# First norm, DFT stage, kernel spectrum and convolution slices put into one list schedule, with the tables' second half by quarters

## The chip, the cores and the metric

The kernel runs on one core of a Trainium2 chip. Times are device microseconds (us) of one execution; the time of a kernel is the median over its runs. A profiled execution gives a trace beside its time; positions in it are in us from the start of its span.

## What is computed

Four layers are added to a residual `x` of 2048 tokens by 512 channels, in bf16: a state-space convolution (A), a dilated sliding attention (B), A again and B again, each on a layer-normed input and each with the same weights in both rounds.

```python
def _A_ref(u, A_re, A_im, B_re, B_im, C_re, C_im, log_dt, Dskip):
    ...
    P = jnp.exp(logdA[:, :, None] * l[None, None, :])
    K = jnp.einsum("dn,dnl,dn->dl", Cc, P, dB).real
    ...
    Yf = Uf * Kf[None, :, :, :]
    ...
    y = (lambda x, *d: x.transpose(*d))(y, 0, 2, 1) + u * Dskip[None, None, :]
    return y
...
x = A_u
x = x + _A_ref(_layernorm(x, axis=-1), ...)
x = x + _B_ref(_layernorm(x, axis=-1), B_wqkv, B_wo)
x = x + _A_ref(_layernorm(x, axis=-1), ...)
x = x + _B_ref(_layernorm(x, axis=-1), B_wqkv, B_wo)
return x
```

A is a long convolution by FFT with a kernel `K` of 2048 lags for each channel, a sum over 128 complex modes. B has 32 heads of 16, each token looking at 8 keys, 2 tokens apart.

## The kernel before

**Front: the convolution's kernel (`kgen`, from L345).** `_kgen_ladder` raises the modes' factors to the powers 1, 2, 4 to 2048 (`Lb`). From these VectorE multiplies out two tables, `V` (32 multiples of 8 lags) and `U` (21 offsets): for each complex product four multiplications and two sums (`cmul`, L322). The 512 channels are done in two halves, the half in two blocks of 128 channels (blocks 0 to 3). In the first half TensorE adds the products up in PSUM (`psadd`, L473 and L474) and ScalarE writes the table back (L475); in the second half VectorE does the sums too. For each block, `products` (L418) multiplies V by U on TensorE (`psk`, four groups of 32 matmuls), ScalarE copies the result to `KT`, and small transfers put it in order (`rows`, eight of 20 KB, L442, for blocks 2 and 3 half of them issued by ScalarE). `spectrum` (L448) multiplies `rows` by a DFT matrix `G` (`psg`, four steps `b` of ten matmuls for each block), ScalarE evicts to `ks`, and SyncE stores it to the DRAM scratch `kt_scratch` (L457, 256 KB each).

**First norm.** ScalarE takes sums and squares of the 16 row groups (`first_norm_stats`, L165), handed out a few at a time by `norm_stats`; four of the squares come behind block 2's evictions. After the last table operation VectorE applies the norm, 16 operations (`first_norm_apply`, L188).

**First convolution (`a_layer`, L240).** `first_stage` (L218) is the first DFT stage: 16 steps of two matmuls (`ps_s`), set in turns with the last spectrum steps by hand, evicted to `Z` by ScalarE and VectorE in turn. Then 16 slices of 32 channels run in a fixed software pipeline (loop at L283): TensorE transposes (`pt`), VectorE evicts (`zt`), TensorE runs the second stage (`xp`), ScalarE evicts (`xc`), VectorE multiplies by the kernel's spectrum (`pab`, L294), TensorE inverts (`vp`), ScalarE evicts to `VT` (L279). A slice's spectrum `Kt` is loaded by SyncE as two transfers of 256 KB into one of four buffers; slice `cg + 4` is issued once the product of slice `cg` has read its buffer. The matrix of the inverse's last stage, `F1T`, has its own tile and is loaded before slice 0. The last lag (`kU`, L304 and L306) comes after the last slice. Then the first attention layer begins with the rows of the result (`y_rows`, `ps_y`).

**Attention (`b_layer`, L677) and the scheduler.** `Plan` (L616) takes operations with an engine, an estimated duration, what they follow and which buffer they take and give back, and emits them at trace time: again and again the operation with the earliest start, the first in the list among equals. An operation counts as done 0.2 us (`LAG`) after its end, for every engine. In the before kernel only `b_layer` is made by it. Each engine then runs its list in that order; semaphores hold it where something is not ready. The second convolution uses `a_layer` again, with `Z` made by the first attention layer's end.

## Time and profile before

| | us |
|---|---|
| runs | 498.71, 503.98, 503.78 |
| median | 503.78 |
| profiled execution, its time | 499.52 |
| its span | 497.7 |

| stretch of the span | from | to | length |
|---|---|---|---|
| loads, ladder, start of the tables | 0 | 42.0 | 42.0 |
| tables, first half | 42.0 | 64.6 | 22.6 |
| tables, second half | 64.6 | 110.8 | 46.2 |
| first norm applied, first DFT stage, rest of the spectrum | 110.8 | 144.5 | 33.7 |
| slices of the first convolution | 144.5 | 181.2 | 36.7 |
| first attention, with the second layer's DFT stage | 181.2 | 326.4 | 145.2 |
| slices of the second convolution | 326.4 | 363.4 | 37.0 |
| second attention, store | 363.4 | 497.7 | 134.3 |

Busy over the whole span: TensorE 401.0 us (81%), VectorE 421.8 (85%), ScalarE 339.0 (68%). Each engine works through its own list; what an engine waits for is put down to the semaphore that came last. The chain of waits follows the execution back from its last instruction, at each step to what released it. The DMA share is the mean busy share of the core's 16 DMA engines.

### The profile page before, as it was taken

How to read it: one execution, taken by the hardware profiler on the slowest of the kernel's cores; microseconds unless marked ns; L12 is line 12 of the kernel's file. 1: busy time of each engine (PE TensorE's matmuls, PEld its weight loads, DVE VectorE, ACT ScalarE, POOL GpSimd, SP SyncE). 2: the span in 40 equal slices, each digit the busy share in tenths (PEclk: the TensorE clock that was granted, in tenths of full speed). 3: DMA queues.
4: the chain of work that ended last, by engine and by line, in shares of the span. 5: the costliest groups of instructions: out<-in, count | busy, mean ns of one | idle time of the engine just before them, and what ended most of it. 6: DMA issues, size and time to landing. Idle time of an engine off the chain costs nothing.

```text
span 497.7 us, 11589 instructions
## 1 busy us (share of the span) xinstructions
PE 401.0 (81%) x4760; PEld 261.9 (53%) x4760; DVE 421.8 (85%) x842; ACT 339.0 (68%) x571; POOL 4.6 (1%) x19
## 2 busy tenths in 40 slices
PE   2008789959979979999876798779889998957896
PEld 1003366446437844685664565258645674845663
DVE  4999999995458969895999999978788886999980
ACT  5987988665658968768552279769868667733244
POOL 3000000000000000000000000000000000000000
PEclk9999975979999999999995699999999999975699
DMA  8910001633669970037073003529800073080022
GB/s 255 426 81 0 2 1 28 121 63 71 163 151 279 258 209 2 1 88 147 3 151 82 2 3 79 175 78 238 196 1 1 4 159 75 19 199 19 1 85 86
DMA packets 38404, 49.85 MB, mean 100 GB/s; under 512 B 27936, under 2 KB 29216, under 8 KB 37456
## 3 DMA queue, kind: packets, MB, share of 16 engines
q1 hardware_dynamic: 35488, 45.81, 35.6%
q10 hardware_dynamic: 2704, 3.18, 2.6%
q8 instruction: 37, 0.61, 0.5%
q0 software_dynamic: 160, 0.13, 0.1%
q14 instruction: 15, 0.12, 0.1%
HBM read 30.67 MB, written 6.29 MB: 74 GB/s over the span
## 4 chain that ended last, share of the span: by engine, by line
PE 37%; DVE 21%; DMA 10%; ACT 5%; issue 3%; ACTq 1%; SPq 1%; DVEq 0%
DVE prodqk L836 9%; PE ps_qk L808 7%; DMA Kt<-kt_scratch 6%; DVE prodpv L959 5%; PE ps_o L989 5%; PE po L966 4%; DMA V<-c_zero 4%; PE psg L451 3%; PE ps_v L862 3%; DVE pab L294 2%; ACT xc L287 2%; PE ps_y L317 2%; PE ps_y L313 1%; PE pt_x L793 1%; PE Lp L848 1%
## 5 line engine op out<-in xcount | busy, mean ns | idle before, releaser
L836 DVE TENSOR_TENSOR prodqk<-qT,kT 128x1024 bf16<-128x1024 bf16 (+3 forms) x176 | 83.0, 537 | 4.8 <-ACT kT L810 2.6
L959 DVE TENSOR_TENSOR prodpv<-V,Lsb 128x1024 bf16<-128x1024 bf16 (+2 forms) x128 | 79.6, 680 | 4.9 <-DMA V<-c_zero 3.2
L808 PE MATMUL ps_qk<-xnT,wqk 128*128 128x512 bf16 x256 | 60.9, 379 | 0.0
L966 PE MATMUL po<-halves,prodpv 128*128 128x64 bf16 x1024 | 50.2, 208 | 8.6 <-DVE prodpv L959 6.0
L966 PEld LDWEIGHTS <-prodpv 128*128 128x128 bf16 x1024 | 42.8, 107 | 19.4 <-DVE prodpv L959 12.3
L294 DVE TENSOR_TENSOR pab<-xc,Kt 128x2048 bf16<-128x2048 bf16 x32 | 39.2, 1224 | 8.8 <-DMA Kt<-kt_scratch 6.8
L451 PE MATMUL psg<-G,rows 128*128 128x512 bf16 x160 | 39.8, 408 | 6.1 <-DMA rows<-KT 6.1
L473 PE MATMUL psadd<-cp,sb_ident 128*128 128x512 bf16 (+3 forms) x48 | 18.1, 378 | 31.8 <-DVE cp L332 28.7
L848 PE MATMUL Lp<-sb_bones,prodqk 128*128 128x8 bf16 x1024 | 32.6, 167 | 11.6 <-DVE prodqk L836 11.2
L848 PEld LDWEIGHTS <-prodqk 128*128 128x128 bf16 x1024 | 30.7, 97 | 17.5 <-DVE prodqk L836 14.5
L277 PE MATMUL vp<-sb_IC,pab 128*128 128x128 bf16 x512 | 33.9, 219 | 3.5 <-DVE pab L294 3.5
L279 ACT CAST VT<-vp 128x1024 bf16<-128x1024 f32 x32 | 32.5, 1016 | 6.1 <-PE vp L277 6.1
L287 ACT CAST xc<-xp 128x1024 bf16<-128x1024 f32 x32 | 32.6, 1020 | 5.7 <-PE xp L210 5.7
L808 PEld LDWEIGHTS <-wqk 128*128 128x128 bf16 x256 | 23.4, 97 | 22.8 <-issue 0.5
L332 DVE TENSOR_TENSOR cp<-Vtab,L 128x896 bf16<-128x896 bf16 (+6 forms) x64 | 34.1, 596 | 0.4 <-PE psadd L474 0.4
L989 PE MATMUL ps_o<-wo_t,oT 128*128 128x512 bf16 x128 | 33.0, 379 | 0.0
L277 PEld LDWEIGHTS <-pab 128*128 128x128 bf16 x512 | 29.8, 98 | 5.4 <-DVE pab L294 4.7
L764 DVE BATCH_NORM_STATS2 ln_stats<-X 128x6 f32<-128x512 bf16 x44 | 28.6, 677 | 4.6 <-ACT X L1021 4.6
L978 ACT CAST oT<-po 128x512 bf16<-128x512 f32 x32 | 17.3, 586 | 21.2 <-PE po L966 21.1
L451 PEld LDWEIGHTS <-rows 128*128 128x128 bf16 x160 | 16.4, 103 | 27.8 <-issue 10.8
L862 PE MATMUL ps_v<-wv,xnT 128*128 128x256 bf16 x256 | 30.9, 272 | 0.0
L332 DVE TENSOR_TENSOR cp<-Utab,L 128x256 bf16<-128x256 bf16 (+4 forms) x60 | 29.3, 548 | 0.9 <-PE psadd L474 0.8
(152 smaller groups left out, 752.5 us busy)
## 6 DMA issues: line engine op xcount, KB each, us to landing
Kt<-kt_scratch SPq DMA_DIRECT2D x64, 256.0 KB
V<-V SPq DMA_DIRECT2D x22, 256.0 KB
G<-c_G SPq DMA_DIRECT2D x4, 1280.0 KB
kt_scratch<-ks SPq DMA_DIRECT2D x16, 256.0 KB
X<-in_A_u_dram SPq DMA_DIRECT2D x4, 512.0 KB
F1Tsb<-c_F1T SPq DMA_DIRECT2D x2, 1024.0 KB
V<-V SPq DMA_DIRECT2D x4, 441.0 KB
F1sb<-c_F SPq DMA_DIRECT2D x1, 1024.0 KB
```

The lines of the kernel that those rows point to most:

```text
L277: nc.tensor.matmul(vp[:, g, :], pab[:, g, ab, :], IC[:, ab, :], start=(ab == 0), stop=(ab == 1))
L287: nc.scalar.copy(xc[:].rearrange("q g o l -> q (g o l)"), xp)
L294: last = nc.vector.tensor_tensor(pab[:], xc[:].to_broadcast([128, 8, 2, 128]), kts[cg][:], ALU.mult)
L332: nc.vector.tensor_tensor(prod[i, r].rearrange("n (h e t) -> n h e t", h=hn, t=2), a(r), m[:, i].unsqueeze(2).to_broadcast([128, hn, e, 2] ...
L451: mms = [nc.tensor.matmul(ps[:, hf, :], rows[:, t, :], Gt[b][:, t, hf * 512:(hf + 1) * 512], start=(t == 0), stop=(t == 4)) for t in range ...
L808: nc.tensor.matmul(t.ps[:], wqk[:, ct, f0:f0 + 128], xnT[g][:, ct, :], start=(ct == 0), stop=(ct == 3))
L836: nc.vector.tensor_tensor(b.pr[:, u:u + 2 * n, a, :], cols(qT[i][:, ja * 128:(ja + n) * 128]), cols(kT[i][:, k0:k0 + n * 128]), ALU.mult)
L848: nc.tensor.matmul(t.Lp[:, w, u % 2, u // 2, :], b.pr[:, u].rearrange("f a q -> f (a q)"), bones[:], start=True, stop=True)
L862: nc.tensor.matmul(t.ps[:, jj, :], xnT[jp // 2][:, ct, c0:c0 + 128], wv[:, ct, fp * 256:(fp + 1) * 256], start=(jj + ct == 0), stop=(jj == ...
L959: nc.vector.tensor_tensor(t.p2[:, 0:nj, :].rearrange("p j (d h) -> p j d h", d=DH), m.V2[i // 2][:, c, r0:r0 + nj, f0:f0 + 128].rearrange( ...
L966: nc.tensor.matmul(po[jj // k][:, jj % k, c - cs[0], :], t.p2[:, jj, :], fold, start=(c == cs[0] and w == 0 and jj % k == 0), stop=(c == c ...
L989: nc.tensor.matmul(t["ps"][:], m.oT[:, ft, j * 128:(j + 1) * 128], wo_t[:, ft, :], start=(ft == 0), stop=False)
```

## The change

The functions `kgen` and the first use of `a_layer` become one function, `front`; `a_layer`'s second use becomes `second_conv`.

- **One list.** From the first half's fifth table step on, everything up to the first convolution's last slice is put into a `Plan`: table steps, products, rows, spectrum, stores, the first norm, the DFT stage, Kt loads, slices, `F1T`, last lag, and the loads of the attention's weights. Hand-made turns are gone. An operation can have a rank; among equal starts the lowest rank goes first. The products (`psk`) of blocks 1 to 3, the norm's applies and the DFT stage's first half share one rank, behind block 0's operations and ahead of block 1's spectrum, of all that follows for blocks 2 and 3, and of the second half's tables; slice `cg` has 100000 + 1000 `cg`, and block 3's four spectrum steps the ranks of slices 4, 6, 8 and 10.
- **Quarters.** In the second half of the tables U_4, U_2 and U_2048 are done for the half; U_1, U_256, U_1024 and U_512 for each block, followed by that block's V. The V16 step is cut in two for each block.
- **Engines.** Half of the norm's applies go to ScalarE. `Z` is made in two halves of 256 channels: the first evicted by ScalarE alone, the second by ScalarE or VectorE as the list finds it. So are `zt`, `xc` and `VT` of the slices.
- **Memory.** U of the first half and one product buffer lie in an arena; after the last reader, the normed rows and the first half of `Z` take it, and in the attention layers `oT` takes the place of `Z`. The slices' buffers, `VT` and the second half of `Z` take the tables' memory after block 3's last product (`done`). All four `G` tiles lie where the ladder's work was. `Kt` has three buffers in the first convolution, four in the second. `F1` and `F1T` share one buffer: `F1T` is loaded after the DFT stage (first convolution: after Kt load 9; second: after Kt load 5), and `F1` once more in the first attention layer.
- **Scheduler.** `Plan` counts an operation as done at its end for the same engine and after the lag for others; a lag can be given (3.0 for Kt loads and stores, 2.4 for rows). This holds for the attention layers too.

```diff
@@ Plan @@
-    def add(self, eng, us, fn, after=(), take=None, drop=()):
+    def add(self, eng, us, fn, after=(), take=None, drop=(), lag=None, rank=None):
...
+    def seen(d, eng):
+
+        return d["end"] + (0.0 if d["eng"] == eng and d["lag"] == Plan.LAG else d["lag"])
...
-        taken, left = {}, list(self.ops)
+        taken, left = {}, sorted(self.ops, key=lambda o: (o["rank"], o["k"]))
@@ first norm @@
-def first_norm_apply(nc, st, Xg, Ng):
-    for j in range(NJ):
-        nc.vector.tensor_scalar(Ng[j // 4][:, j % 4, :], Xg[j // 4][:, j % 4, :], st["rstd"][:, j:j + 1],
-                                st["nb"][:, j:j + 1], ALU.mult, ALU.add)
+    return [plan.add(dict(ACT=0.71) if j % 2 else dict(DVE=0.324), None, lambda eng, j=j: apply(eng, j), [o, room], rank=rank) for j in range(NJ)], sums
@@ slices @@
-        for cg in range(4):
-            load_k(cg)
...
+        k = plan.add("SP", 1.3, load, [room] + stored(cg), take=("Kt", m.kts), lag=3.0, rank=rank)
...
+        a = plan.add("PE", 0.46, turn, [room] + ready(cg), take=PT, rank=rank)
+        b = plan.add(dict(ACT=0.93, DVE=0.61), None, turned, [a], take=("zt", 3), drop=[a], rank=rank)
+        c = plan.add("PE", 0.44, second, [b], take=PX, drop=[b], rank=rank)
+        d = plan.add(dict(ACT=0.92, DVE=1.15), None, spectrum, [c], take=("xc", 2), drop=[c], rank=rank)
+        e = plan.add("DVE", 1.14, product, [d, k], take=("pab", 4), drop=[d, k], rank=rank)
...
+        f = plan.add("PE", 1.03, inverse, [e], take=PS, drop=[e], rank=rank)
...
+        ends.append(plan.add(dict(ACT=0.92, DVE=1.15), None, inversed, [f], drop=[f], rank=rank))
+    for cg in range(16):
+        rank = 100000 + 1000 * cg
+        slice32(cg)
+    for cg in range(14):
+        inverses[cg]["after"].append(seconds[cg + 2])
@@ second_conv @@
+        m = SimpleNamespace(z=lambda h: Z[:, h * 64:(h + 1) * 64], kts=4)
...
+        plan.add("SP", 0.65, load_f1t, loads[5:6], rank=0)
+        last_lag(nc, plan, m, C, Ng, ends[11:12])
@@ front: tables, second half @@
-        U = u_start(1)
-        for step in (U_4, U_2, U_1, U_256, U_1024, U_512, U_2048):
-            u_last = u_mul(1, U, *step)
...
+        products(0)
+        rank1 = len(plan.ops)
+        products(1)
+        start = [plan.add("DVE", 0.35, lambda: u_start(1))]
+        for st in (U_4, U_2, U_2048):
+            start = dve_step(u_mul(1, cp[:], *st), start)
+        for q, (h0, h1) in enumerate(quarters):
+            o = start
+            for st in (U_1, U_256, U_1024, U_512):
+                o = dve_step(u_mul(1, cp[:], *st, h0, h1), o)
...
+            for k in (2, 4, 8):
+                o = dve_step(v_mul(1, cp[:], k, h0, h1), o)
+            for i in range(2):
+                e = (h1 - h0) // 2
+                o = dve_step(v_mul(1, cp[:], 16, h0 + i * e, h0 + (i + 1) * e), o)
+                got["tab", 2 + q, 2 * i] = got["tab", 2 + q, 2 * i + 1] = o
+            if q:
+                rank_g.update({(3, b): 100000 + 1000 * (4 + 2 * b) for b in range(4)})
+            products(2 + q)
@@ front: products and spectrum in the list @@
+                p = plan.add("PE", 1.08, pe, need + (got["rows", c - 2] if c > 1 else []), take=PS if q % 2 else PX, rank=rank1 if c else None)
...
+                p = plan.add("PE", 2.16, pe, got["moved", c], rank=rank, take=PS, drop=[r0] if b == 3 else ())
+                o = plan.add("ACT", 0.92, evict, [p], take=("ks", 2), drop=[p], rank=rank)
+                got["stored", c].append(plan.add("SP", 0.65, store, [o], drop=[o], lag=3.0, rank=rank))
@@ front: norm, memory, DFT stage @@
+        room = plan.add("-", 0.0, arena, [p for ps, _ in half0 for p in ps] + [got["psk", c, q][0] for c in range(2) for q in range(4)])
+        normed, sums = first_norm(nc, plan, C, Xg, Ng, room, cpp.tile([128, D], BF, name="junk"), rank1)
...
+        done = plan.add("-", 0.0, tables_done, [got["psk", 3, q][0] for q in range(4)] + sums)
...
+                p = plan.add("PE", 0.23, pe, [normed[j]] + ([done] if hf else []), take=PX if j % 3 == 2 else PT, rank=None if hf else rank1)
...
+                got["Z", hf].append(plan.add(dict(ACT=act_us(512), DVE=0.68) if hf else dict(ACT=act_us(512)), None, evict, [p], drop=[p], rank=None if hf else rank1))
+        m.z = lambda h: m.Z[h]
+        loads, ends = conv_slices(nc, plan, m, C, kt_dram, lambda cg: got["Z", cg // 8], lambda cg: got["stored", cg // 4], done)
+        last_lag(nc, plan, m, C, Ng, [done] + got["rows", 3])
...
+        plan.add("SP", 0.65, f1t, s1 + [loads[9]])
@@ b_layer @@
-            m.oT = m.vo.tile([128, 4, S], BF, name="oT")
+            m.oT = C["arena2"].rearrange("f (i s) -> f i s", i=4)
+            if not last_layer:
+                C["F1"] = C["f1"].tile([128, NJ, 2, 128], BF, name="F1", tag="F1")
...
+        if not last_layer:
+            plan.add("SP", 0.65, lambda: nc.sync.dma_start(C["F1"][:], C["F1_h"].ap()), [y_end])
```

## The prediction

> **What bounds the kernel now.** I first read the busy time by stages, since the change rewrites only the work up to the first convolution's end (181.2 us); the rest it touches only through the scheduler's rule and two table loads. The columns are the stretch, its length, then busy time of TensorE, its weight loads, VectorE (DVE), ScalarE (ACT) and GpSimd, the granted clock, the DMA share and GB/s.
>
> ```profile
> 64.60:110.80 46.20, 38.46 (x463) 25.52 (x463) 46.17 (x101) 33.08 (x63) 0.00 (x0) 0.77 0.31 58
> 110.80:144.50 33.70, 30.85 (x249) 15.46 (x250) 16.00 (x35) 20.74 (x26) 0.21 (x1) 0.96 0.53 123
> 144.50:181.20 36.70, 30.75 (x417) 25.15 (x416) 31.13 (x36) 31.37 (x33) 0.00 (x0) 1.00 0.97 259
> ...
> 326.40:363.40 37.00, 30.93 (x416) 25.10 (x417) 31.16 (x36) 30.34 (x32) 0.00 (x0) 1.00 0.73 172
> ```
>
> From 64.6 to 110.8 VectorE is full: it multiplies out the tables' second half. From 110.8 to 144.5 VectorE has 16.0 of 33.7 us; nothing else is ready for it. In both convolutions (third and fourth line) no engine is full, but the DMA share of the first is 0.97. The chain of waits says what ends last there:
>
> ```profile
> 108.54 1.88 DMA rows<-KT
> ...
> 110.76 5.84 PE psg L451 x20
> ...
> 126.19 2.16 PE psg L451 x10
> ...
> 142.49 2.16 PE psg L451 x10
> ...
> 159.09 1.24 DVE pab L294
> 160.34 0.51 SPq L259
> ...
> 160.91 6.57 DMA Kt<-kt_scratch
> ...
> 177.81 1.24 DVE pab L294
> ```
>
> After the tables the chain runs over the rows' transfer, then through TensorE's spectrum (psg, 2.16 us for ten matmuls) and the first DFT stage in turns, and from 159 through Kt loads: a product (pab) frees a buffer, the next load is issued and lands 6.57 us later. How fast that stream can be, the windows of ten microseconds show:
>
> ```profile
> 90.00:100.00 10.00, 10.00 (x48) 4.52 (x47) 10.00 (x22) 5.77 (x7) 0.00 (x0) 1.00 0.67 132
> ...
> 160.00:170.00 10.00, 9.45 (x134) 7.85 (x132) 8.58 (x11) 9.63 (x12) 0.00 (x0) 1.00 1.04 261
> 170.00:180.00 10.00, 7.82 (x113) 6.50 (x111) 7.84 (x8) 8.42 (x9) 0.00 (x0) 1.00 1.04 284
> ```
>
> At a full share (1.04) Kt loads move 261 GB/s (the third line has the weights in it too); so 512 KB, one slice, take 2.0 us, the pace of the products (pab at 161.98 to 177.81: eight slices in 15.8). In the first line only spectrum stores ran, one per 2.16 us at a share of 0.67: 1.45 us of all engines each.
>
> **The change part by part.** All is worked against the profiled execution: span 497.7, time 499.52. The median of the three runs is 503.78, 4.26 above, so the difference found is taken off the median.
>
> *Tables by quarters.* Four U steps and each V16 step are cut in two: (4 + 2) x 6 = 36 more instructions on VectorE. Their fixed cost, from start to start in VectorE's timeline:
>
> ```profile
> 55.86 2.36 DVE L332 TENSOR_TENSOR cp<-Vtab,L 128x960 bf16<-128x960 bf16 x4 [0.36 <-PE psadd L474]
> 58.14 1.96 DVE L332 TENSOR_TENSOR cp<-Utab,L 128x768 bf16<-128x768 bf16 x4
> ...
> 91.37 4.35 DVE L332 TENSOR_TENSOR cp<-Vtab,L 128x1920 bf16<-128x1920 bf16 x4
> 95.65 2.22 DVE L341 TENSOR_TENSOR Vtab<-cp 128x1920 bf16<-128x1920 bf16 x2
> ```
>
> 960 columns take (58.14 - 55.86)/4 = 0.57 us, 1920 take (95.65 - 91.37)/4 = 1.07, so a cut costs 2 x 0.57 - 1.07 = 0.07, 36 cuts 2.5 us, on the path because VectorE is full. The first norm's sixteen applies (5.26 us on VectorE at 114.77, 0.33 each) come earlier and half of them go to ScalarE; they rank ahead of the tables, so 8 x 0.33 + 0.4 for the two small operations = 3.0 lands inside VectorE's full stretch. Tables end at 110.8 + 2.5 + 3.0 = 116.3. The last two of block 3's four psk groups (0.54 x 2 each in TensorE's timeline from 116.6) follow: 118.5. Call this D. Everything of the convolution (Kt buffers, VT, second half of Z) lies in memory handed over at D.
>
> *After D, transfers.* Nothing of Kt is loaded before D; in the kernel before, four slices were there when the first product ran at 147.67. From D on the engines have to move: Kt 8.39 MB at 261 GB/s = 32.1; F1T 1.05 MB at 391 GB/s (the rate at 150 to 152) = 2.7; block 3's four stores 5.8; block 2's stores, of which I take half as still to come, 2.9 (0 to 5.8); rows of block 3 1.1 (the share 0.22 over 75 to 80). Sum 44.6. The first bytes land 1.9 after issue (the rows' transfer). Kt has three buffers in place of four. If a load took its 6.57 us whatever else is queued, a turn would be 1.24 + 0.51 + 6.57 = 8.3 and a slice 2.77, a loss of 0.76 x 13 = 9.9; if 6.57 is the queue behind three other slices (3 x 2.0), the loss is near 0. The second reading is nearer, so 3. From the last product to the last VT eviction 177.81 to 181.22 = 3.4. End: 118.5 + 1.9 + 44.6 + 3 + 3.4 = 171.4, against 181.2: 9.8 earlier.
>
> The Trainium skill's page "DMA: Bandwidth & Descriptors" (section "Where 436 GB/s comes from") puts the ceiling at 435 GB/s. By it, an estimate, Kt would take 19.3 and not 32.1 us, and the transfers would bind nothing. The trace reaches 427 GB/s in the first loads (12 to 16 us), but Kt's 261 comes at a full share, and the measurement decides.
>
> *After D, engines.* TensorE: 16 slices at 0.45 + 0.43 + 0.89 (pt, xp, vp in its timeline) = 28.3, block 3's spectrum 8.6, the second half of the DFT stage 16 x 0.23 = 3.7, half of block 2's spectrum 4.3: 44.9, to 163.4. ScalarE and VectorE share their evictions: xc and VT 32 x 0.92 = 29.4, spectrum evictions 6 x 0.92 = 5.5, row issues 2.6, block 3's KT 2.5; pab 16 x 1.15 = 18.4, zt 16 x 0.6 = 9.6, kU 2.5, Z 16 x 0.6 = 9.6; together 80, 40 each, to 158.5 if they balance, with a tenth lost 162.5. Both lie below 171.4, so the transfers hide them; if a slice of Kt cost 1.5 and not 2.0 us, TensorE would be next.
>
> *Second convolution.* F1 and F1T now share one buffer. Before, F1T was issued when transfers were idle, ahead of the Kt stream:
>
> ```profile
> 316.59 0.36 SPq L301 DMA_DIRECT2D F1Tsb<-c_F1T  x1
> 330.73 23.38 SPq L259 DMA_DIRECT2D Kt<-kt_scratch  x24
> ```
>
> Now it is queued after the sixth Kt load, inside a stream whose products wait for DMA from 345 on. It adds its own 2.7 (0 if the stream has slack, 2.9 by the shares of 316 to 324). kU, 2.5 on VectorE, moves into the waits there: no gain, since the chain goes from VT.
>
> *Free of cost.* F1 is loaded again after the first convolution: 2.7 us of transfer at a share under 0.1 (190 to 220), needed at 305. G waits for the ladder's memory, to about 36; 5.2 MB are 12.5 us at 420 GB/s, needed at 80.95. The weights (2.2 MB) still follow the last Kt load. Each would cost its length if that cover went.
>
> *The scheduler's rule.* An operation on the same engine now counts as ready with no 0.2 lag, so both attention stages get another order. No row prices that. VectorE idles 14.6 of 145.2 and 24.2 of 134.3 us there; a twelfth of it each way is 3. I take 0, as the instructions are the same.
>
> Sum: -9.8 + 2.7 = -7.1: 492.4 for the profiled execution, 503.78 - 7.1 = 496.7 as a median.
>
> **The rivals.** *Full overlap.* Three buffers lose nothing, block 2's stores lie before D, F1T finds slack: 118.5 + 1.9 + 41.7 + 3.4 = 165.5, so -15.7: 488.1. For it: the share was 1.0 for 30 us on end. Against: three buffers, and ScalarE and VectorE both near full.
>
> *D comes late.* On ScalarE the first norm's applies and the first Z evictions rank ahead of block 2's spectrum evictions, and the last products share two PSUM buffers (psS) with that spectrum. If ScalarE's squares end at 103 (112.6 before), the square root (1.6), 8 x 0.73 and 16 x 0.49 (like operations of the attention, start to start) follow to 118.3, then the first ks to 119.2, and only then the second of the last four psk groups finds a buffer: three groups of 1.08, D = 122.4, with all of block 2's stores behind it: 122.4 + 1.9 + 47.5 + 3 + 3.4 = 178.2, so -3.0 + 2.7 = -0.3: 503.5. For it: the ranks, and ScalarE's 33.1 of 46.2 us in the first line of the stages, to which Z and the applies are added. Against: the psk themselves rank ahead of block 2's psg, and may have the buffers first.
>
> *Stores block the loads.* SyncE issues in order. A spectrum store that waits for its eviction holds every Kt load behind it, and the list is made with a Kt load of 1.3 + 3.0 us, not 6.57, so its order can be off there:
>
> ```profile
> SPq L457 <- ACT ks L455: 22.8, 9, 5.5
> ```
>
> That is 2.5 us for a store, over nine of them, with Kt loads queued behind. Before, these waits fell where no product needed Kt. With six stores after D: 6 x 2.5 = 15 us, 186.4 in place of 171.4: +5.2 + 2.7 = +7.9: 511.7, slower than before. It decides from 7.1/6 = 1.2 us a store. Against: block 3's spectrum may run as soon as TensorE idles, ahead of its place. The Trainium skill's page "DMA: Bandwidth & Descriptors" (section "Queues, rings and completion order") adds that descriptors in one engine's ring are consumed in ring order; no row here shows the order inside a ring.
>
> **How the numbers follow.** 1% (5 us) is about what a measurement can tell from no change. The forecast gets 0.38 (0.27 faster by over 1%, 0.11 within: its margin is only 2 us), full overlap 0.23 (faster), late D 0.17 (0.14 within, 0.03 slower), blocked loads 0.22 (0.19 slower, 0.03 within). Faster 0.50, same 0.28, slower 0.22. The likeliest case alone runs from 492 to 501 (three buffers 0 to 6, scheduler's rule). The range reaches from 487, just past full overlap, to 508, which leaves out most of the blocked loads beyond 1.9 us a store.
>
> **What would show it.** Right: the last psk by 118 to 120, the first Kt issue right behind it, DMA share near 1.0 from 122 to 168, the last VT at about 171; pab idle put down to Kt; F1T issued after 331 and the second convolution ending near 366. Full overlap: the same with VT at 165. Late D: block 2's ks behind Z evictions, and the last psk past 121. Blocked loads: SyncE's queue waiting for ks evictions after D while the DMA share falls. I am wrong if Kt loads run well above 261 GB/s, if VectorE's tables end past 120, or if an attention stage changes by more than 3 us.

## The result and the profile after

The changed kernel takes 519.66 us (median of 519.21 to 524.44), the kernel before, run beside it, 501.38 us: ratio 1.0387, 95% interval 1.0291 to 1.0482. I had predicted 496.7 us, between 487 and 508, and faster. It is slower, and outside the range. The profiled execution has a span of 518.3 us, 20.6 more than before. Where they lie (us; the third column is what the prediction's terms make of each mark):

| | before | predicted | after |
|---|---|---|---|
| tables end | 110.8 | 116.3 | 123.7 |
| last psk of block 3 | 121.0 | 118.5 | 127.0 |
| last VT, first convolution | 181.2 | 171.4 | 190.5 |
| first attention, length | 145.2 | 145.2 | 147.6 |
| second convolution, length | 37.0 | 39.7 | 43.1 |
| last attention and store, length | 134.3 | 134.3 | 137.1 |
| span | 497.7 | 490.6 | 518.3 |

The stages after, read as those of before: stretch, its length, busy time of TensorE, its weight loads, VectorE, ScalarE and GpSimd, granted clock, DMA share, GB/s.

```profile
68.10:123.70 55.60, 44.39 (x581) 28.27 (x582) 54.41 (x147) 45.64 (x77) 0.00 (x0) 0.94 0.31 58
123.70:146.80 23.10, 22.09 (x160) 12.60 (x163) 8.69 (x23) 10.06 (x14) 0.21 (x1) 0.85 0.57 126
146.80:190.50 43.70, 31.43 (x410) 25.23 (x415) 28.98 (x32) 32.06 (x33) 0.00 (x0) 0.96 0.82 221
...
338.10:381.20 43.10, 34.77 (x409) 29.36 (x417) 31.00 (x35) 31.01 (x33) 0.00 (x0) 0.86 0.64 172
```

The tables' second half (first line) is 55.6 us in place of 46.2, with VectorE nearly as full as before (54.41 us of it). Then follow 23.1 us with 8.69 of VectorE and a DMA share of 0.57. The slices (third line) have a share of 0.82 where the kernel before had 0.97. The second convolution (fourth line) is 6 us longer at a granted clock of 0.86. The chain of waits through the front (start, length, what):

```profile
123.76 0.65 PE psk L517 x15
...
126.05 0.87 PE psk L517 x16
...
127.72 5.88 PE psg L559 x18
...
146.82 0.46 PE pt L214 x8
...
170.58 1.24 DVE pab L231
171.83 0.52 SPq L206
172.39 8.66 DMA Kt<-kt_scratch
181.18 1.24 DVE pab L231
```

The first psk groups take 0.65 us and the last 0.87. From 126.96 to 146.82 the chain is TensorE but for 1.43 us of Z evictions on VectorE: spectrum (psg) and the second half of the DFT stage (ps_s) by turns, and only then the first slice (pt). From 150 on it runs in triples: a product (pab) gives a buffer back, the next load is issued (SPq, 0.51), it lands (DMA Kt). One landing took 8.66 us; the megabyte of F1T had been issued at 170.54, just ahead. The windows of ten microseconds show what the stream did meanwhile:

```profile
140.00:150.00 10.00, 9.31 (x72) 5.71 (x72) 6.10 (x16) 5.03 (x6) 0.00 (x0) 1.00 0.62 131
150.00:160.00 10.00, 8.97 (x122) 7.23 (x122) 7.79 (x10) 8.48 (x9) 0.00 (x0) 1.00 0.71 175
...
170.00:180.00 10.00, 6.14 (x78) 4.37 (x77) 5.48 (x6) 7.37 (x8) 0.00 (x0) 1.00 0.99 287
```

I had written that the share would be near 1.0 from 122 to 168. It is 0.62 in the first of these windows (stores, nearly no Kt) and reaches 0.99 only after 170. SyncE's issues from the last psk on show the same (start, length, what; a slice's Kt is two transfers):

```profile
126.95 1.22 SPq L206 DMA_DIRECT2D Kt<-kt_scratch  x2
...
135.24 2.51 SPq L206 DMA_DIRECT2D Kt<-kt_scratch  x4
139.50 8.80 SPq L568 DMA_DIRECT2D kt_scratch<-ks  x4
151.67 18.83 SPq L206 DMA_DIRECT2D Kt<-kt_scratch  x18
```

### The profile page after: what moved, and what is told of

It is laid out like the page before. It is cut to its first block, busy times and chain, and to the rows that moved or that the text cites. A ratio compares the mean times of both kernels' runs of the same rounds, so it can differ in the third digit from the quotient of the medians.

```text
span 518.3 us, 11674 instructions
## 1 busy us (share of the span) xinstructions
PE 405.3 (78%) x4739; PEld 270.7 (52%) x4792; DVE 422.7 (82%) x872; ACT 346.7 (67%) x594; POOL 4.6 (1%) x19
## 4 chain that ended last, share of the span: by engine, by line
DVE 35%; PE 34%; DMA 12%; ACT 10%; issue 5%; SPq 3%; DVEq 0%
DMA Kt<-kt_scratch 8%; PE ps_qk L957 7%; DVE cp L327 7%; DVE prodqk L985 6%; DVE prodpv L1108 6%; PE po L1115 5%; DMA V<-V 4%; PE ps_o L1138 3%; PE psg L559 3%; DVE pab L231 2%; SPq L1035 2%; DVE Vtab L337 2%; DVE Utab L337 2%; PE ps_y L282 2%; ACT junk L166 1%
## 5 line engine op out<-in xcount | busy, mean ns | idle before, releaser
L1115 PE MATMUL po<-halves,prodpv 128*128 128x64 bf16 x1024 | 53.0, 215 | 16.1 <-DVE prodpv L1108 14.4
L1115 PEld LDWEIGHTS <-prodpv 128*128 128x128 bf16 x1024 | 46.4, 112 | 28.2 <-DVE prodpv L1108 19.3
L237 PE MATMUL vp<-sb_IC,pab 128*128 128x128 bf16 x512 | 37.0, 231 | 16.2 <-DVE pab L231 15.9
L237 PEld LDWEIGHTS <-pab 128*128 128x128 bf16 x512 | 33.3, 104 | 24.9 <-DVE pab L231 20.4
L997 PEld LDWEIGHTS <-prodqk 128*128 128x128 bf16 x1024 | 32.6, 97 | 12.4 <-DVE prodqk L985 8.8
L959 ACT CAST qT<-ps_qk 128x512 bf16<-128x512 f32 x32 | 18.6, 589 | 24.8 <-PE ps_qk L957 24.3
L450 PE MATMUL psadd<-arena_k,sb_ident 128*128 128x512 bf16 (+3 forms) x26 | 10.2, 391 | 29.8 <-DVE arena_k L327 26.9
L1138 PE MATMUL ps_o<-wo_t,arena 128*128 128x512 bf16 x120 | 31.3, 379 | 0.6
L327 DVE TENSOR_TENSOR cp<-Vtab,L 128x960 bf16<-128x960 bf16 (+4 forms) x56 | 26.9, 538 | 3.6 <-PE psadd L451 1.6
L1127 ACT CAST arena<-po 128x512 bf16<-128x512 f32 x32 | 17.5, 587 | 18.0 <-PE po L1115 17.5
```

What stands on the lines that cost most here:

```text
L237: nc.tensor.matmul(t.vp[:, g, :], t.pab[:, g, ab, :], IC[:, ab, :], start=(ab == 0), stop=(ab == 1))
L327: self.nc.vector.tensor_tensor(self.part(i, r).rearrange("n (h e t) -> n h e t", h=self.hn, t=2), self.a(r), self.m[:, i].unsqueeze(2).to_ ...
L997: nc.tensor.matmul(t.Lp[:, w, u % 2, u // 2, :], b.pr[:, u].rearrange("f a q -> f (a q)"), bones[:], start=True, stop=True)
L1115: nc.tensor.matmul(po[jj // k][:, jj % k, c - cs[0], :], t.p2[:, jj, :], fold, start=(c == cs[0] and w == 0 and jj % k == 0), stop=(c == c ...
L1138: nc.tensor.matmul(t["ps"][:], m.oT[:, ft, j * 128:(j + 1) * 128], wo_t[:, ft, :], start=(ft == 0), stop=False)
```

## The experiments

Each kernel was run beside the kernel before on the same chip. The last six columns are read from its profiled execution, in us:

| kernel | ratio to before (95% interval) | tables end | last psk | last VT | first attention | second convolution | last stage |
|---|---|---|---|---|---|---|---|
| before | 1 | 110.8 | 121.0 | 181.2 | 145.2 | 37.0 | 134.3 |
| changed | 1.0387 (1.0291 to 1.0482) | 123.7 | 127.0 | 190.5 | 147.6 | 43.1 | 137.1 |
| before_new_rule | 1.0089 (1.0054 to 1.0125) | 110.8 | 121.6 | 182.1 | 148.3 | 36.5 | 137.6 |
| after_old_rule | 1.0253 (1.0184 to 1.0322) | 123.1 | 126.9 | 189.3 | 144.4 | 42.3 | 134.3 |
| after_prod_order | 1.0289 (1.0215 to 1.0364) | 120.3 | 122.6 | 183.3 | 146.5 | 42.4 | 138.7 |
| after_dft_late | 1.0339 (1.0270 to 1.0408) | 124.1 | 127.0 | 187.6 | 148.1 | 43.7 | 137.7 |
| after_f1t_last | 1.0306 (1.0227 to 1.0385) | 124.3 | 127.5 | 188.3 | 146.4 | 39.0 | 138.8 |
| after_ku_last | 1.0387 (1.0312 to 1.0462) | 124.0 | 127.2 | 191.6 | 149.9 | 40.1 | 138.2 |
| after_kts4 | 1.0360 (1.0290 to 1.0430) | 123.7 | 126.8 | 187.1 | 147.1 | 42.1 | 141.7 |
| after_psk_late | 1.0431 (1.0324 to 1.0538) | 121.6 | 127.1 | 194.9 | 145.8 | 43.2 | 136.9 |
| after_half_kt | 1.0082 (1.0042 to 1.0123) | 123.4 | 127.0 | 183.3 | 146.3 | 34.9 | 137.2 |
| after_pool | 1.0356 (1.0322 to 1.0390) | 123.1 | 126.7 | 190.4 | 146.6 | 43.8 | 136.9 |
| four_parts | 1.0049 (1.0014 to 1.0085) | 120.2 | 122.6 | 182.1 | 144.2 | 39.1 | 135.9 |
| four_dft | 1.0044 (1.0008 to 1.0079) | 120.5 | 122.8 | 180.4 | 144.4 | 37.3 | 136.1 |
| four_kts4 | 0.9980 (0.9943 to 1.0018) | 120.7 | 123.0 | 179.1 | 144.8 | 38.5 | 135.3 |
| six_parts | 1.0008 (0.9969 to 1.0046) | 120.1 | 122.5 | 179.8 | 146.3 | 38.8 | 135.0 |
| base_norm_act | 1.0163 (1.0085 to 1.0240) | 118.0 | 125.5 | 186.8 | 143.1 | 36.9 | 136.4 |
| base_whole_u | 1.0075 (1.0038 to 1.0111) | 119.2 | 123.0 | 184.5 | 146.4 | 37.1 | 134.0 |
| base_psk_split | 0.9993 (0.9961 to 1.0025) | 120.1 | 123.8 | 178.8 | 144.8 | 38.1 | 135.0 |
| six_pool | 0.9973 (0.9945 to 1.0001) | 121.0 | 124.7 | 179.4 | 145.9 | 39.3 | 134.0 |

A stage that a kernel leaves alone moves by 1 to 2 us from one execution to the next, at most by 5 (the last stage with the new rule: 136.9 to 141.7), so the table is read by the stage that an edit touches. The three kernels with the changed front as it is (changed, after_old_rule, after_ku_last) have the last VT at 189.3 to 191.6; a gain of 2 us there, out of one execution each, is near that spread.

### The scheduler's rule alone, added and taken away

```diff
@@ before_new_rule: Plan of the kernel before, replaced by that of the changed kernel @@
-            o["end"] = end + self.LAG
+    def seen(d, eng):
+        return d["end"] + (0.0 if d["eng"] == eng and d["lag"] == Plan.LAG else d["lag"])
@@ after_old_rule: Plan of the changed kernel; b_layer makes its own with same=False @@
+    def __init__(self, clocks, same=True):
-        return d["end"] + (0.0 if d["eng"] == eng and d["lag"] == Plan.LAG else d["lag"])
+        return d["end"] + (0.0 if self.same and d["eng"] == eng and d["lag"] == Plan.LAG else d["lag"])
```

> The kernel before, with nothing changed but the planner's rule in both attention stages: an operation on the same engine counts as ready with no lag of 0.2 us. Theory 'rule' (the two attention stages of the changed kernel grew by 2.4 and 3 us because the rule gives them another order): first attention 147 to 148 us long in place of 145.2, the last stage about 137 in place of 134.3, whole time about 5 us longer, ratio near 1.010. Rival 'place' (the stages grew because of what the changed convolutions leave behind, such as where oT lies and the second load of F1, and the rule is worth nothing): attention stages within 1 us of before, ratio near 1.000.

> The changed kernel with the old rule (0.2 us of lag on the same engine too) in the two attention stages alone; the front and the second convolution keep the new one. Theory 'rule': first attention back to about 145, the last stage to about 134, whole time about 5 us shorter than the changed kernel, near 514. Rival 'place': no change, near 519.

The rule costs 3.1 and 3.3 us in the kernel before, and taking it out of the changed kernel gives back 3.2 and 2.8: as the theory had it, both ways, and the rival falls. Over all twenty executions the ten with the rule have a mean of 147.3 and 138.1 us in the two stages, the ten without 145.0 and 135.0. How it works shows at one place on ScalarE. First the kernel before (start, length, engine, line, operation, idle time before it):

```profile
217.59 0.58 ACT L868 CAST V<-ps_v 128x512 bf16<-128x512 f32 x1 [0.21 <-PE ps_v L862]
218.07 0.34 ACT L906 COPY Lsb<-never 1x32 bf16<-1x32 bf16 x2
218.47 0.59 ACT L868 CAST V<-ps_v 128x512 bf16<-128x512 f32 x1
219.08 0.24 ACT L906 COPY Lsb<-never 1x64 bf16<-1x64 bf16 x1
```

and the same place with the new rule:

```profile
219.88 1.21 ACT L912 COPY Lsb<-never 1x16 bf16<-1x16 bf16 x7
221.11 2.28 ACT L874 CAST V<-ps_v 128x512 bf16<-128x512 f32 x4
```

One of seven mask copies follows the other on the same engine. With the lag of 0.2 us the list put a V eviction between them; without it all seven follow at once, and four V evictions (and the copies of V behind them) come later. VectorE's products with V then wait 13.2 us for V in two places of before_new_rule, where the kernel before had 3.2.

### The order of products and sums

```diff
@@ after_prod_order: dve_step @@
-            for i in range(2):
-                for r in range(2):
+            for i, r in ((0, 0), (1, 0), (1, 1), (0, 1)):
```

> The changed kernel with the four products of each complex multiplication in the tables' second half issued as (0,0), (1,0), (1,1), (0,1), so that no sum and no next product reads what the instruction right before it has written. Theory 'handoff' (VectorE waits out the whole previous instruction where it reads its result, 0.1 to 0.2 us at each of about 40 boundaries, and the written-out order of the changed kernel puts each such read right behind the write): the tables' second half 3 to 4 us shorter, 52 in place of 55.6, and the last psk 3 to 4 us earlier. Rival 'instruction count' (the stage is longer only by the cuts and the norm, and by the ScalarE and TensorE work beside it): no change in that stage, within 0.5 us.

VectorE's timeline at the first steps of the second half, in the changed kernel:

```profile
68.09 1.26 DVE L327 TENSOR_TENSOR cp<-Utab,L 128x256 bf16<-128x256 bf16 x4
69.39 0.64 DVE L337 TENSOR_TENSOR Utab<-cp 128x256 bf16<-128x256 bf16 x2
70.07 1.43 DVE L327 TENSOR_TENSOR cp<-Utab,L 128x512 bf16<-128x512 bf16 x4
```

and with the other order:

```profile
67.28 1.26 DVE L327 TENSOR_TENSOR cp<-Utab,L 128x256 bf16<-128x256 bf16 x4
68.46 0.62 DVE L337 TENSOR_TENSOR Utab<-cp 128x256 bf16<-128x256 bf16 x2
69.12 1.43 DVE L327 TENSOR_TENSOR cp<-Utab,L 128x512 bf16<-128x512 bf16 x4
```

and in the kernel before:

```profile
64.57 1.26 DVE L332 TENSOR_TENSOR cp<-Utab,L 128x256 bf16<-128x256 bf16 x4
65.75 0.62 DVE L341 TENSOR_TENSOR Utab<-cp 128x256 bf16<-128x256 bf16 x2
66.24 1.43 DVE L332 TENSOR_TENSOR cp<-Utab,L 128x512 bf16<-128x512 bf16 x4
```

From the first product to the first sum it was 1.30 us and is 1.18, while the four products take as long as ever; at 512 columns it went from 1.46 to 1.34, at 960 from 2.39 to 2.28. The stage went from 55.6 to 53.0 us, over 21 steps 0.12 each, and every other kernel confirms it: 55.6 in all eight others with the old order of products, 53.0 in every one with the new order whose cuts and norm are as in the changed kernel. (In the kernel before, 1.18 too: there the order was made automatically, the changed list is written out.) The edit leaves a second wait of the same kind. In the kernel before the next product begins while the sum ahead of it still runs (66.24, the sum ends at 66.37); with either written-out order it begins 0.03 us after that sum's end (70.03 and 70.07; 69.08 and 69.12). This happens at 10 of the 20 such places of the stage, once of 14 in the kernel before, and at 0.12 each that is, as an estimate, 1.1 us more; the expectation had it gone, and no run took it out. The tables' end came 3.4 earlier, of which 0.8 was already there when the second half began, which the edit doesn't explain (among the kernels that leave the first half as in the changed one it begins between 67.1 and 68.7). The last psk came 4.3 earlier: 2.3 us behind the tables and not 3.3. TensorE's granted clock stayed at 1.00 there, where it had fallen to 0.50 for 6.8 us: in the changed kernel and seven others without the new order it fell within 2 us of the tables' end. With the new order it did so in none of nine, but in base_whole_u it had fallen 2.8 us ahead of it. The last section has the rows.

### When TensorE begins with the slices

```diff
@@ after_dft_late: second half of the DFT stage, its 16 steps among the slices @@
-                p = plan.add("PE", 0.23, pe, [normed[j]] + ([done] if hf else []), take=PX if j % 3 == 2 else PT, rank=None if hf else rank1)
+                p = plan.add("PE", 0.23, pe, [normed[j]] + ([done] if hf else []), take=PX if j % 3 == 2 else PT, rank=100000 + 450 * j if hf else rank1)
```

> The changed kernel with the rank of the DFT stage's second half set behind the convolution's first slices (16 steps spread over the ranks of slices 0 to 7), so that the first slices run on TensorE while the spectrum and the second half of the DFT stage go on. Theory 'TensorE's order' (VectorE lies idle from the last psk to the first product because TensorE does the whole second half of the DFT stage and block 3's spectrum first): first pt at about 128 in place of 146.8, the last VT of the first convolution 6 to 10 us earlier, whole time near 511. Rival 'transfers' (the Kt stream with three buffers sets the end of the slices, wherever they begin): first pt early, but the last VT within 2 us of 190.5, whole time near 518.

The first pt came at 132.4 and not 146.7, but the last VT only 2.9 us earlier, between the two: 14 us of earlier start, 2.9 of earlier end. The waits of the products changed their name; the busy group of pab in the first convolution (waits in us, times):

```profile
  ACT xc L185: 7.4, 6
  DMA Kt<-kt_scratch: 5.4, 3
```

In the changed kernel it had been 8.8 us for Kt and 0.7 for xc. ScalarE now has spectrum, Z, xc and VT at once, and by these waits is the next to end last.

### What F1T and kU cost

```diff
@@ after_f1t_last @@
-        plan.add("SP", 0.65, f1t, s1 + [loads[9]])
+        plan.add("SP", 0.65, f1t, s1 + [loads[15]])
-        plan.add("SP", 0.65, load_f1t, loads[5:6], rank=0)
+        plan.add("SP", 0.65, load_f1t, loads[15:16], rank=0)
@@ after_ku_last: second convolution @@
-        last_lag(nc, plan, m, C, Ng, ends[11:12])
+        last_lag(nc, plan, m, C, Ng, m.products[15:16])
```

> The changed kernel with F1T loaded after the last Kt load in both convolutions, in place of after the tenth (first) and the sixth (second). Theory 'queued behind F1T' (a megabyte of F1T ahead of Kt loads that products wait for costs its own transfer, about 2.7 us, and the products stand for it): the wait of 4.5 us for Kt at 361 in the second convolution goes and that convolution is 3 to 4.5 us shorter (about 39 in place of 43); in the first one 8.7 us of wait falls to 6 and the last VT comes 1 to 3 us earlier; whole time near 514. Rival 'slack': the products wait for the stream anyway, which moves the same bytes; each convolution within 1 us of before, near 519.

> The changed kernel with the four kU operations of the second convolution behind its last product, as in the kernel before, and not ahead of the last two. Theory 'kU in the way' (2.5 us of VectorE ahead of the last two products): second convolution 2 to 2.5 us shorter, whole time near 517. Rival 'hidden' (the last two products wait for their Kt loads or for xc anyway): within 0.5 us, near 519.5.

In the changed kernel VectorE's timeline of the second convolution had this:

```profile
361.77 1.23 DVE L231 TENSOR_TENSOR pab<-xc,Kt 128x2048 bf16<-128x2048 bf16 x1 [4.49 <-DMA Kt<-kt_scratch]
...
373.09 1.21 DVE L264 TENSOR_TENSOR kU<-arena,klast 1x2048 bf16<-1x2048 bf16 x1
374.33 1.30 DVE L266 TENSOR_TENSOR kU<-kU 1x512 bf16<-1x512 bf16 x3
375.57 2.34 DVE L231 TENSOR_TENSOR pab<-xc,Kt 128x2048 bf16<-128x2048 bf16 x2
```

F1T behind the stream gives 2.2 us in the first convolution. In the second one the clock has to be kept apart: of the kernels whose second convolution is as in the changed one, six began it at half clock, with 42.3 to 43.8 us, and after_kts4 at 1.00, with 42.1. after_f1t_last and after_ku_last also began at 1.00: against 42.1, F1T gives 3.1 us and kU 2.0. The two kernels with both edits that had the full clock (four_dft, base_norm_act) take 37.3 and 36.9, so the two add, and nothing is left to explain against the 37.0 of before; the six others with both began at half clock and take 37.1 to 39.3. Yet after_ku_last as a whole is no faster (1.0387 both times; its first attention, left alone, was 2.3 us longer), so kU's price in the time is not shown.

### Buffers, bytes and queues of the slices

```diff
@@ after_kts4: first convolution @@
-        m = SimpleNamespace(kts=3)
+        m = SimpleNamespace(kts=4, pabs=3)
...
-            t.pab = m.fwork.tile([128, 8, 2, 128], BF, name="pab", tag="pab", bufs=4)
+            t.pab = m.fwork.tile([128, 8, 2, 128], BF, name="pab", tag="pab", bufs=m.pabs)
@@ after_half_kt: both convolutions @@
+            if cg % 2:
+                t.Kt = m.half
+                return
...
@@ after_pool: spectrum stores of blocks 2 and 3 @@
-                    nc.sync.dma_start(dst.rearrange("k d l -> d k l"), k.ks[:].rearrange("d (k l) -> d k l", l=128))
+                    (nc.gpsimd if c > 1 else nc.sync).dma_start(dst.rearrange("k d l -> d k l"), k.ks[:].rearrange("d (k l) -> d k l", l=128))
```

> The changed kernel with four Kt buffers in the first convolution, the room taken from the products (three pab buffers in place of four, in the first convolution alone). Theory 'round trip' (with three buffers a buffer's turn of product, issue and landing sets the pace): last VT of the first convolution 4 to 8 us earlier. Rival 'bytes' (after the tables' end the transfers alone fill the time, whatever the buffers): last VT within 1.5 us of 190.5. My prediction had taken 3 us for it, between 0 and 9.9.

> The changed kernel with Kt loaded for every second slice only, in both convolutions; the slice after it multiplies by the same Kt, so half of the spectrum is left out of the result and 4.2 MB of each convolution's loads fall away. Theory 'transfers' (my prediction's: after the tables' end the bytes set the first convolution's end, 44.6 us of them): 16 us of transfer gone, last VT 8 to 16 us earlier than 190.5; the second convolution, whose products waited 4.5 us for Kt, 3 to 4.5 us shorter. Rival 'TensorE and ScalarE' (the second half of the DFT stage, block 3's spectrum and the evictions set it): last VT within 3 us of 190.5.

> The changed kernel with the spectrum stores of blocks 2 and 3 issued by GpSimd and not by SyncE; nothing else. Rival of the prediction 'stores block the loads' (Kt loads stand behind stores that wait for their evictions, 2.5 us each): the last VT 5 to 15 us earlier than 190.5. Theory 'buffers, not the queue' (the Kt loads after the first three slices wait for buffers that the products free, and these begin at 150, so the queue's order costs nothing by itself): last VT within 2 us of 190.5, whole time near 519.

The fourth buffer gives 3.4 us at the last VT, half of the bytes 7.2 in the first convolution and 8.2 in the second; in the first convolution both lie just under the lower end that the theory had, in the second the gain is twice what it had (3 to 4.5), of which about 1 is the clock, at 1.00 throughout. Half of the bytes, from 150 to 170:

```profile
150.00:170.00 20.00, 19.52 (x278) 16.87 (x281) 19.35 (x23) 19.22 (x21) 0.00 (x0) 1.00 0.62 169
```

TensorE, VectorE and ScalarE are all busy for more than 19 of the 20 us: halving the bytes is worth 7.2 of the 43.7 us that the slices take, and behind the transfers these three engines are full. Stores on GpSimd's queue change nothing (190.4): SyncE's order is not what held the loads.

### The tables' end

```diff
@@ after_psk_late (base_psk_split cuts block 0's groups in two instead) @@
-                need = got["tab", c, q] + (got["psk", c, q - 1] if q else [])
+                need = got["tab", c, q] + (got["psk", c, q - 1] if q else half0[-1][0] if c == 0 else [])
@@ base_norm_act @@
-    return [plan.add(dict(ACT=0.71) if j % 2 else dict(DVE=0.324), None, lambda eng, j=j: apply(eng, j), [o, room], rank=rank) for j in range(NJ)], sums
+    return [plan.add(dict(ACT=0.71), None, lambda eng, j=j: apply(eng, j), [o, room], rank=rank) for j in range(NJ)], sums
@@ base_whole_u @@
-        for st in (U_4, U_2, U_2048):
+        for st in (U_4, U_2, U_2048, U_1, U_256, U_1024):
-            for st in (U_1, U_256, U_1024, U_512):
+            for st in (U_512,):
```

> The changed kernel with block 0's products on TensorE (psk) held back until the tables' first half has had its last sum. Theory 'TensorE in front' (whole groups of psk, 0.9 to 1.1 us each, stand ahead of the sums psadd that free the product buffers, and VectorE waits 3.2 us for them between 50 and 65): the first half of the tables ends at 64.6 to 65.5 in place of 68.1, and the second half's end and the last psk come 2 to 3 us earlier. Rival 'ScalarE' (the sums wait for evictions and the first norm's sums on ScalarE whatever TensorE does): the first half still ends after 67.

> The best version so far with block 0's psk groups on TensorE cut in two, so that sums of the first half can go between them. Theory 'TensorE in front': half of the 3.2 us of VectorE's waits for psadd go, the first half of the tables ends near 66.5 and all behind it 1.5 us earlier. Rival 'ScalarE': no change within 0.5 us.

> The best version so far (old rule in the attention, order of products, F1T last, kU last, four Kt buffers) with all sixteen applies of the first norm on ScalarE, none on VectorE. Theory 'VectorE is full': eight applies of 0.33 us leave its stretch, tables end 2.6 us earlier (117.5 in place of 120.1), the last VT as much. Rival 'ScalarE is next' (its evictions wait behind eight more applies of 0.73): tables end earlier, but the last psk or the last VT no earlier than before, 179.

> The best version so far with three of the four cut U steps of the tables' second half whole again (18 instructions fewer on VectorE), ahead of both quarters. By 0.07 us a cut, as the prediction had it, 1.3 us: tables end at 118.9 in place of 120.1. If a cut costs more, 0.15 with its handoffs, 2.7 us. Against it: block 2's psk start later, by the second quarter's share of those steps, which may cost the spectrum behind them.

Block 0's psk held back, the first half ends at 65.95 and not 68.09 (start of the first product of the second half), so about 2 of its 3.5 us are TensorE's (2.1 against this one execution, 1.2 against the earliest of the kernels that leave that half alone, 67.1); but the last psk comes no earlier (127.1), the work put off comes later (first pt 151.7), and the last VT is 4.4 us late. Cut in two, the groups give 0.6 (67.70 to 67.14), which is within that spread (six_pool, with the same cut, begins at 68.03), and no time. The last two each shorten the second half, from the 53.0 us of four_kts4 to 50.2 and 51.6, and lose it at once. Without VectorE's applies TensorE does spectrum between block 3's psk groups and ends them 2.5 us later than in four_kts4. With three U steps whole (18 instructions fewer, 1.4 us of the stage, so 0.076 each) block 2's products begin later, two more of its spectrum steps (2.16 us each) fall behind the last psk, and the slices begin at 146.5 in place of 140.7. So the three cuts cost 1.4 us, and the last VT is 5.4 us earlier with them (179.1 against 184.5). How much of either loss is the clock is open: four_kts4 has it at 1.00 from 90 us on, base_norm_act at 0.50 from 104.0 to 114.2, and base_whole_u from 116.4 to 126.6, where a psk group takes 1.02 us and not 0.66.

### Together

> The changed kernel with four edits together: the old rule in the attention stages, products and sums in the order that keeps reads away from writes, F1T after the last Kt load, kU behind the last product of the second convolution. Theory 'separate causes' (each edit acts in its own stage, so the gains add: 6.7 + 4.9 + 4.1 + 0 us by the ratios measured one by one): ratio to the kernel before near 1.008, about 504 to 505. Rival 'one bound' (a gain in the front is taken back in the transfers after the tables, or by the attention): above 1.017.

> The four edits and the DFT stage's second half behind the first slices. By the sum of single gains another 2.4 us: ratio near 1.003. If the transfers set the slices' end once F1T is out of their way, the same as the four edits, 1.008.

> The four edits and four Kt buffers with three pab buffers in the first convolution. By the sum of single gains another 1.4 us: ratio near 1.005. If F1T's place had already removed that wait, no gain over the four edits.

> All six edits. By the sum of single gains 19.5 us off the changed kernel: ratio 1.000. First convolution's last VT at about 177 by the gains seen in the front (7.2 + 2.2 + 2.9 + 3.4 us off 190.5 would be 174.8 if all of them added); attention stages 145 and 134, second convolution 37 to 39. If the front's gains share one bound (the transfers after the tables), VT stays at 180 or later and the ratio above 1.006.

> All six edits, block 0's psk groups cut in two, and the spectrum stores of blocks 2 and 3 issued by GpSimd. Theory 'ring' (a store issued behind Kt loads on the same queue leaves after them, and with two ks buffers ScalarE's next eviction waits for it, 6.8 us at 137, with all its other evictions behind): the wait goes, last VT at 173 to 176 in place of 179.8, ratio near 0.99. Rival 'shared engines' (the transfers share the same sixteen engines, whatever queue issues them): a wait of 4 us or more stays, last VT within 2 us of 179.8, ratio 1.000.

four_parts takes the first four of these edits (rule, order, F1T, kU); single ratios summed gave 1.007, measured is 1.0049 (1.0014 to 1.0085), as it would be with separate causes. four_dft adds the DFT stage's place, four_kts4 the buffers, six_parts both. four_kts4 gives back all that the change had lost: 0.998, not told apart from before. DFT stage and buffers together gain nothing on one of them (1.0008). In six_parts ScalarE stood for a store that had been issued behind eight Kt transfers (four slices):

```profile
143.58 1.01 ACT L566 CAST ks<-psg 128x1024 bf16<-128x1024 f32 x1 [6.77 <-DMA kt_scratch<-ks]
```

With the stores on GpSimd's queue (six_pool, which also has block 0's groups cut in two) this wait is gone. The Trainium skill's page "DMA: Bandwidth & Descriptors" (section "Queues, rings and completion order") has a ring of its own for each queue on every engine, and the engines going round between rings; this pair of runs agrees with it, where the prediction had no row. It doesn't single out the ring, since the store was also issued late: its eviction ended at 133.06, and SyncE came to it at 137.05, behind the eight. From the last psk to the last VT it is 54.7 us in place of 57.3; but the last psk came 2.2 later in that execution and VT stayed at 179.4, where the theory had 173 to 176. Its ratio is 0.9973 with 1.0001 as upper end. No version is shown to beat the kernel before.

## Why the prediction was wrong, step by step

Against its own sum (span 490.6) the changed kernel is 27.7 us late: 8.4 to the last psk, 10.7 from there to the last VT, 2.4 and 2.8 in the attention stages, 3.4 in the second convolution. Two steps of the sum made most of it: the tables' end, which left out what the new order costs, and the transfers, which were added up from the last psk on.

- **Tables, 116.3 foreseen, 123.7 measured; the step "36 cuts 2.5 us".** The cuts (at 0.076 each, 2.7) and the norm (3.0 foreseen, 3.1 measured, 90.8 to 94.0) were right. What failed is that they were all: missing were the first half, which I took as unchanged (3.5, of which about 2 are shown to be TensorE's groups in front of the sums; the rest is open), the order inside a product (2.6), and the ten sums that the next product waits for (1.1, read from the trace alone). I had costed instructions by start to start inside a row, where no one reads what was just written. With these terms the sum comes to 123.8.
- **The last psk, 2.2 us behind the tables; measured 3.3.** The clock, at 0.50 there. In after_prod_order, at 1.00, it took 2.3.
- **From there to VT, 52.9 foreseen, 63.5 measured; the step "transfers 44.6".** The bytes were right and the rate nearly: at a share of 1.04 four_kts4 moves 246 GB/s, where I had 261. The error was to let the stream run from the last psk on. Three slices were issued by 137.8 and filled the buffers, and the first product comes at 150.4, because TensorE does spectrum and DFT stage first: the next Kt load was issued at 151.67, and for 13.9 us there was none. I had set TensorE's 44.9 us against the transfers as if both could run side by side from the start. That the gap costs its length is not shown: with the first product 14 us earlier (after_dft_late) the last VT came 2.9 earlier, since the products then waited for ScalarE; and with half of the bytes 7.2. So neither the transfers nor the engines alone set this stretch. Three buffers, 3 us in my sum, cost 3.4. Of the 10.7 us the single edits give back 3.4 (buffers), 2.9 (TensorE's order), 2.2 (F1T last) and 2.9 (the stretch of after_prod_order, 60.6, with the full clock); they share some of it, and each is one execution. With every edit 54.7 us are left, 1.8 above my sum.
- **Second convolution, 2.7 for F1T; measured 6.1 in all:** F1T 3.1, kU 2.0, the half clock about 1. F1T's mechanism and size were right. kU I had costed at nothing, in waits that VectorE has there; but two products stood behind it, and they are the last.
- **The scheduler's rule, 0 taken of plus or minus 3; measured 4.5 to 6.7 us** (0.89% in the kernel before; in the changed one 1.0387 less 1.0253, 1.34%). "The instructions are the same" was true and no reason: a twelfth of the idle time each way had been a guess, and it was too small.
- **Free items.** F1 loaded again, G later, weights later: in after_old_rule the attention stages are 144.4 and 134.3 us, where before they were 145.2 and 134.3, and no matmul of the spectrum waited for G, so they cost nothing, as I had it.
- **The rivals.** Stores that block the loads (0.22, on the side that came true) fell by after_pool. D did come late, but over VectorE's tables and the clock, not over ScalarE and psS. Full overlap (0.23) fell too: the last psk is at 127.0, and the share over the slices is 0.82. Slower came by none of the rivals, but by terms that were not in the sum or put at nothing (first half, order of product and sum, kU, the rule, the clock) and by one that was wrongly overlapped. Of the signs of being wrong that I had named, the tables' end past 120 is the one that came true.

## What to carry to other kernels

When an order is written out by hand, count besides the instructions who reads what was just written, and what a list now lets pass in one block: the first came free from an automatic order, the second from a lag in the list, and they cost 2.6 and 4.5 to 6.7 us here. A stream of transfers can't be summed from the moment its memory is free; it runs only as far as its buffers reach until the first consumer starts, so look for that consumer's start on its own engine. An edit that shortens one stretch (a norm taken off a full engine, cuts undone) has to be read at the next common end: here both were lost again by the last VT.

## What the hardware showed that I had not expected

TensorE's granted clock falls to half after a short slack and stays there for several microseconds. At the start of the second convolution, changed kernel, then before (columns as in the stages above):

```profile
338.10:340.10 2.00, 2.00 (x17) 1.80 (x18) 0.80 (x2) 0.00 (x0) 0.00 (x0) 0.50 0.00 0
340.10:342.10 2.00, 2.00 (x16) 1.56 (x15) 0.90 (x2) 1.01 (x1) 0.00 (x0) 0.50 0.00 0
```

```profile
326.40:328.40 2.00, 1.66 (x22) 1.30 (x23) 1.29 (x2) 0.00 (x0) 0.00 (x0) 1.00 0.00 0
```

Sixteen transposes took 1.89 us there and 1.07 in the kernel before, and the first product came 5.2 us after the first transpose, not 3.1. In windows of one microsecond the clock was 0.50 from 321.8 to 325.2 in the kernel before, and in the changed one from 124.6 to 131.4 and from 332.8 to 343.0: 3.4, 6.8 and 10.2 us. Ahead of the first and the last TensorE had been without matmuls for some two microseconds; ahead of 124.6 it had been busy for 0.52 and 0.45 of the two microseconds from 122 and wholly busy for the 0.6 just before. The 3.41 us ahead of the fall at 124.59 and of the one at 332.81, changed kernel:

```profile
121.18:124.59 3.41, 2.38 (x70) 2.18 (x68) 2.49 (x5) 1.42 (x2) 0.00 (x0) 1.00 0.41 82
...
329.40:332.81 3.41, 1.48 (x6) 0.41 (x5) 3.12 (x9) 2.56 (x6) 0.00 (x0) 1.00 0.00 0
```

The Trainium skill's page "TensorE: Matmul & The Clock Gate" (Part 1) says that the clock is judged in free-running windows of about 3.4 us, half rate after an idle one, full rate after a busy one. The three lengths agree with one, two and three windows. That the window before is idle holds at none of these falls: TensorE was busy for 1.45 us of the 3.41 ahead of 321.8, for 1.48 ahead of 332.8 and for 2.38 ahead of 124.6, and lost the clock all the same.

A VectorE sum that reads what the product right before it wrote costs about 0.12 us more than one whose latest operand is two instructions old (21 steps, 2.6 us in all): it starts 0.03 us after the end that the trace has for that product, the other 0.08 us ahead of it.
